# Seven products in the last dense chunk, and expert weight sums stored as plain blocks

## The chip, the cores and the metric

The kernel runs on one core of a Trainium2 chip. The metric is the device time of one execution in microseconds (us), as the median of several runs. The engines are TensorE (PE, matmuls), VectorE (DVE), ScalarE (ACT), GpSimd (POOL) and SyncE (SP, which here issues nearly all DMAs). Each engine works through its own list of instructions in order.

## The reference

Everything is fp32. An attention with packed keys is followed by a dense layer pair and a mixture of eight experts with a gating that is normalised in eight rounds. Sizes: 2304 tokens (4 batches of 576), model width 512, dense width 2048, 8 experts of width 1024.

```python
p_packed = sm_attn(p, k, v)                  # 4 x 8 heads, 32 packed keys
x = sm_attn(q, p_packed, p_packed)           # -> 2304 x 512
h = x @ w_in                                 # 512 -> 2048
x = (h * (1.0 / (1.0 + np.exp(-h)))) @ w_out # 2048 -> 512
logits = x @ w_gate
P = np.exp(logits - logits.max())
for _ in range(8):
    P /= P.sum(1, keepdims=True) + 1e-09
    P /= P.sum(0, keepdims=True) + 1e-09
    P *= N / E
for e in range(E):
    out += P[:, e:e + 1] * (np.maximum(x @ w1[e], 0.0) @ w2[e])
```

## The kernel before

**Precision.** PE multiplies numbers of a shortened fp32 format. Each operand is split into a high part (a cast on ACT) and a rest (a subtraction on DVE); that pair is the helper `split`, L145 and L146. A product of two operands is then three matmuls: high by high, high by rest, rest by high.

**Dense stage.** The dense width is cut into four chunks c of 512. Within a chunk the four batches b follow each other. For each batch `make_u` computes u (PE, L251) and splits it into Uh (ACT, L637) and Ul (DVE, L638). `gemm1` multiplies it with the attention's factors a2h and a2l: units g of 2 x 6 = 12 matmuls of 288 columns (L652), silu on ACT into `graw` (L683), and a split into the buffer `ring` (L684, L685). `gemm2_wide` multiplies ring by the split weights woh and wol: 24 tiles per chunk (2 batch pairs x 3 column ranges x 4 row blocks), each of 12 matmuls of 384 columns (L736). Half of the tiles are seeded with the running sum x2a or x2b by ACT (L721) and copied out by ACT (L741); the other half are added to x2 by DVE (L743). `convs` loads the next chunk's raw weights (win, rawin, ct, rawout; L519 on SP) and converts them on ACT and DVE (L528 to L546): the custom operation L539 ends the conversion of a w_out block. The work of this stage has the order of the code on PE, DVE and ACT (`tc.manual_schedule`).

**Expert weights.** The expert stage has 48 steps: 3 token groups by 16 weight blocks (8 experts x 2 halves). Group 0 (256 tokens) is computed plainly. Groups 1 and 2 (1024 tokens each) use Strassen and Winograd's scheme: seven products in place of eight, on quarter blocks of w1 and w2, of which four need sums of quarters. `pre_w1` computes the four sums S_1 to S_4 of each of the 16 weight blocks on DVE (L851) out of two raw blocks r of 512 KB, splits them into tiles po, and stores each with both parts (512 KB) to the DRAM tile w1d (L841, on SP). It is a generator: `pump_pre` takes `RATE[c]` pieces of it per unit of weight, where a g unit counts 0.8 and a wide tile 2 + 2/15. In the same way `pump_conv` takes pieces of the conversion. The generator runs through chunks 1, 2 and 3; `pre0` then splits the first step's tokens (xs) and weights (w1l, w2l). Behind chunk 3 comes lg, the gating product (L1235).

**Groups 1 and 2.** `moe_step` interleaves up products (12 matmuls of 512 columns, L1201, accumulators X, Z and Y) with down products d (12 matmuls, L1153) of the step before: 7 slots of 24 matmuls per step. `w1_get` fetches the weights of the product that comes `AHEAD` = 3 slots later: for the products 1, 2 and 4 the raw quarter `rb` (256 KB, loaded ahead by `w1_block`) is split, for 6, 7, 5 and 3 the stored pair is loaded from w1d as one DMA of 512 KB, tile w1l.

Of the kernel before, what the change touches and what calls it, by code (L numbers as in the profile page):

```python
# [28 lines left out]
RATE = {1: 36 / 64, 2: 36 / 64, 3: 41 / 53}  # L29
CONV = 0.6  # L30
TW = 384
LATE = 3
AHEAD = 3

# [71 lines left out]
def fused_kernel(  # L106
# [134 lines left out]
    win, wout = {}, {}  # L241
# [270 lines left out]
    def conv2(c, kind, j):  # L512
# [393 lines left out]
    def w1_block(s, p, name="rb"):  # L906
        _, e, fh = steps[s]
        t = st[name].tile([128, 2, 256], F32, tag=name, name=f"rb{s}_{p}")
        r, c = 256 * (p != 1), FH * fh + 256 * (p == 4)
        nc.sync.dma_start(t, w1[e, r:r + 256, c:c + 256].rearrange("(c p) f -> p c f", p=128))  # L910
        raw1[s, p] = t

    def w1_get(s, p):
        if p not in (1, 2, 4):
            wf[s, p] = get(w1d, s, p)
        else:
            t = unit([128, 2, 2, 256], F32R, f"w1f{s}_{p}")
            split(t[:, 0], t[:, 1], raw1.pop((s, p)))
            wf[s, p] = t
# [642 lines left out]
```

## Time and profile before

| what | value |
|---|---|
| time, median of 3 runs | 1785.59 us (1784.74 to 1787.44) |
| time of the profiled execution | 1784.47 us |
| its span, first to last instruction | 1782.7 us |
| chunks 1 to 3 of the dense stage end at | 369.96 us |
| last g unit and wide tiles of chunk 3 | 354.28 to 369.96 us |

The span is what the trace covers; 1.8 us of the execution's time lie around it. All starts in the rows below are counted from the start of the span. A group of rows in the trace joins instructions of one line, engine, operation and tile; its mean is the duration of one instruction, and since neighbours on an engine overlap a little, the distance between two starts can be shorter than the mean.

### The profile page before, as it was taken

The numbers are of one execution on the slowest core, as the hardware profiler recorded it, in microseconds if no ns is written. First come the engines' busy times: TensorE is split into PE (matmuls) and PEld (weight loads), VectorE is DVE, ScalarE is ACT, GpSimd is POOL, SyncE is SP. The second block draws the span as 40 slices with busy tenths as digits, with TensorE's granted clock in tenths as the row PEclk, the third lists the DMA queues.
The fourth block names the chain that finished last, engine by engine and source line by source line (L and its number), as shares of the span: only waits on it lengthen the run. The fifth ranks groups of instructions, "written<-read, shape, count | busy, mean of one in ns | idle before, by whom it ended". The sixth has DMA issues, their size and how long they took to land.

```text
span 1782.7 us, 25352 instructions
## 1 busy us (share of the span) xinstructions
PE 1764.3 (99%) x9564; PEld 1506.0 (84%) x9564; DVE 1438.8 (81%) x1918; ACT 1066.4 (60%) x1694; POOL 1.0 (0%) x8
## 2 busy tenths in 40 slices
PE   7999999999999999999999999999999999999998
PEld 4999999989998888888888888888888888888887
DVE  7868796759676988999889999887777777777778
ACT  6776675644454666665666666656555555555555
POOL 0000000000000000000000000000000000000000
PEclk9999999999999999999999999999999999999999
DMA  9326676875664655465544455964454444445432
GB/s 353 139 95 214 245 263 249 329 258 172 221 209 161 229 181 183 160 203 187 197 163 171 172 187 195 324 221 166 156 174 164 155 154 148 170 155 171 148 130 94
DMA packets 141498, 341.75 MB, mean 192 GB/s; under 512 B 11952, under 2 KB 49472, under 8 KB 140480
## 3 DMA queue, kind: packets, MB, share of 16 engines
q1 hardware_dynamic: 141376, 340.14, 54.7%
q8 instruction: 75, 1.23, 0.3%
q14 instruction: 47, 0.39, 0.1%
HBM read 256.66 MB, written 83.44 MB: 191 GB/s over the span
## 4 chain that ended last, share of the span: by engine, by line
PE 95%; DVE 2%; DMA 2%; ACT 1%; issue 0%; SPq 0%; DVEq 0%; ACTq 0%
PE d L1153 34%; PE X L1201 20%; PE Z L1201 10%; PE g2w L736 8%; PE g L652 5%; PE Y L1201 5%; PE u L1046 5%; PE d L1065 4%; PE g L704 3%; DMA v<-in_v_dram 1%; PE u L251 1%; DMA kq<-in_kT_dram 0%; PE pp L367 0%; PE s L251 0%; PE lg L1235 0%
## 5 line engine op out<-in xcount | busy, mean ns | idle before, releaser
L146 DVE TENSOR_TENSOR lo<-hb,hi 128x1024 fp32r<-128x1024 f32 x224 | 273.5, 1221 | 33.4 <-ACT hi L145 32.3
L1153 PE MATMUL d<-hi,w2f 128*128 128x512 f32 x896 | 294.2, 389 | 0.0
L1201 PE MATMUL X<-xf,w1l 128*128 128x512 f32 x1152 | 276.9, 389 | 0.0
L145 ACT CAST hi<-hb 128x1024 fp32r<-128x1024 f32 x224 | 235.4, 1052 | 64.9 <-PE d L1153 59.6
L1201 PEld LDWEIGHTS X<-xf,w1l 128*128 128x128 f32 x1152 | 216.2, 188 | 44.9
L1161 ACT COPY M<-d 128x512 f32<-128x512 f32 x234 | 137.4, 589 | 143.9 <-PE d L1153 140.7
L1165 DVE TENSOR_TENSOR M<-d,M 128x512 f32<-128x512 f32 x204 | 140.1, 687 | 100.8 <-PE d L1153 100.8
L1153 PEld LDWEIGHTS d<-hi,w2f 128*128 128x128 f32 x896 | 168.1, 188 | 34.9
L1153 PE MATMUL d<-lo,w2f 128*128 128x512 f32 x448 | 174.3, 389 | 0.0
L1153 PE MATMUL d<-hi,w2l 128*128 128x512 f32 x512 | 167.8, 389 | 0.0
L736 PE MATMUL g2w<-ring,woh 128*128 128x384 f32 x576 | 147.6, 337 | 0.0
L1149 ACT COPY d<-M 128x512 f32<-128x512 f32 x216 | 127.1, 589 | 21.1 <-DVE M L1165 19.7
L1153 PE MATMUL d<-hi,w2g 128*128 128x512 f32 x384 | 125.7, 389 | 0.0
L1153 PEld LDWEIGHTS d<-hi,w2l 128*128 128x128 f32 x512 | 96.1, 188 | 20.3 <-ACT d L1149 0.4
L736 PEld LDWEIGHTS g2w<-ring,woh 128*128 128x128 f32 x576 | 102.9, 188 | 8.6 <-issue 7.5
L1208 ACT COPY cp<-X 128x512 f32<-128x512 f32 x128 | 74.7, 583 | 47.2 <-PE X L1201 47.1
L1153 PE MATMUL d<-lo,w2l 128*128 128x512 f32 x256 | 99.6, 389 | 0.0
L1153 PEld LDWEIGHTS d<-lo,w2f 128*128 128x128 f32 x448 | 84.1, 188 | 17.5
L1201 PE MATMUL Y<-xf,w1f 128*128 128x512 f32 x384 | 97.3, 389 | 0.0
L736 PE MATMUL g2w<-ring,wol 128*128 128x384 f32 x288 | 96.3, 334 | 0.0
L1046 PE MATMUL u<-xs,w1h 128*128 128x256 f32 x512 | 94.4, 285 | 0.0
L145 ACT CAST w1f<-rb 128x512 fp32r<-128x512 f32 x96 | 59.8, 624 | 55.8 <-PE d L1153 41.0
(219 smaller groups left out, 3469.0 us busy)
## 6 DMA issues: line engine op xcount, KB each, us to landing
r<-in_moe_w_dram SPq DMA_DIRECT2D x128, 512.0 KB, 4.0
w1l<-w1d SPq DMA_DIRECT2D x128, 512.0 KB, 4.0
w1d<-po SPq DMA_DIRECT2D x64, 512.0 KB, 4.5
w2d<-w2f SPq DMA_DIRECT2D x64, 512.0 KB, 4.0
w2l<-w2d SPq DMA_DIRECT2D x64, 512.0 KB, 3.5
rb<-in_moe_w_dram SPq DMA_DIRECT2D x96, 256.0 KB, 2.6
sb<-in_moe_w_dram SPq DMA_DIRECT2D x48, 256.0 KB, 2.7
pb<-pd SPq DMA_DIRECT2D x16, 512.0 KB, 4.9
```

What stands on the lines that cost most here:

```text
L145: act.copy(out=hi, in_=raw)
L146: eng.tensor_tensor(out=lo, in0=raw, in1=hi.bitcast(F32), op=ALU.subtract)
L652: pe.matmul(ps, lhs[:, fs], rhs, start=(n == 0), stop=(n == 5))
L736: pe.matmul(ps[:, :TW], lhs[:, f % 2, ds], ring[f // 2][:, 2 * (f % 2) + rhs, q], start=(n == 0 and not on), stop=(n == 11), skip_group_ch ...
L1046: pe.matmul(ps[:, i], w[:, k % 2, f], x[:, k], start=(n == 0), stop=(n == 11))
L1065: pe.matmul(ps, h[:, l, f % 2, 128 * tt:128 * tt + 128], w[:, f % 2], start=(fh == 0 and n == 0), stop=(fh == 1 and n == 11))
L1149: act.copy(out=ps, in_=m)
L1153: pe.matmul(ps, w[:, l, c, 128 * d:128 * d + 128], r[:, c], start=(n == 0 and not seed), stop=(n == 5), skip_group_check=seed)
L1161: act.copy(out=m, in_=ps)
L1165: dve.tensor_tensor(m, ps, m, op=ALU.add)
L1201: pe.matmul(ps, w[:, l, c, 128 * i:128 * i + 128], x[:, r, c], start=(n == 0 and p in (1, 7)), stop=(n == 5), skip_group_check=p in (2, 6, ...
L1208: act.copy(out=t, in_=ps)
```

## The change

There are three parts.

1. The second GEMM of the last dense chunk (c = 3) is computed by seven products per batch in place of the wide tiles. `g_unit` leaves silu's result as raw blocks of 288 columns; `forms_a`, `forms_b`, `forms_c` and `h_form` make sums of them and split them into the buffer `ft`, `w_forms` does the same with the weights (tiles wS, from `wz`, the converted blocks that are no longer split). `product` multiplies one form pair with 2 x 6 matmuls of 288 columns, in the accumulators X, Z and Y; X and Z are added to x2 by DVE twice or more as the accumulation goes on, Y is seeded and copied out by ACT.
2. `pre_w1` holds the raw blocks of two steps (tags r1 and rx), and stores each sum S as it is (256 KB) for 13 of the 16 steps; for the steps 0, 1 and 15 (`WHOLE`) it splits and stores pairs as before. It runs in chunks 1 and 2 only.
3. In groups 1 and 2 the products 6, 7, 5 and 3 of those 13 weight blocks get their weights from the stored sum alone: it is loaded as an `rb` block (256 KB, SP), ACT casts it to the high part and writes that part's negative into the rest, then a DMA from GpSimd's queue adds the stored sum to the rest (256 KB, L937). Three `rb` buffers in place of two.

The rates and the raw block without a split:

```diff
-RATE = {1: 36 / 64, 2: 36 / 64, 3: 41 / 53}
-CONV = 0.6
+RATE = {1: 34 / 64, 2: 35 / 64}
+CONV = {1: 0.6, 2: 0.8}
 TW = 384
 LATE = 3
 AHEAD = 3
+WHOLE = (0, 1, 15)
...
+            if c == NC - 1:
+                wz[j] = z.rearrange("p (k f) -> p k f", k=2)
+                return
```

The sums and their use:

```diff
-    def w1_form(s, p, x):
-        if p in (6, 5):
-            t = st["po"].tile([128, 2, 2, 256], F32R, tag="po", name=f"po{s}_{p}")
-        else:
-            t = unit([128, 2, 2, 256], F32R, f"po{s}_{p}")
+    def keep_sum(s, p, x):
+        w1d[s, p] = tc.dram_tile([128, 2, 256], F32, name=f"w1d{s}_{p}")
+        nc.sync.dma_start(w1d[s, p], x)
+    def keep_form(s, p, x):
+        t = unit([128, 2, 2, 256], F32R, f"po{s}_{p}")
         split(t[:, 0], t[:, 1], x)
         put(w1d, s, p, t)
-    def pre_w1(todo, then):
-        load_w1(todo[0], 0)
-        load_w1(todo[0], 1)
-        yield
-        yield
-        for s, nxt in zip(todo, todo[1:] + [then]):
-            forms_ = yield from sums4(s)
-            load_w1(nxt, 0)
-            load_w1(nxt, 1)
-            yield
-            yield
-            for p, x in forms_:
-                w1_form(s, p, x)
+    def pre_w1(todo):
+        for i in range(2):
+            for j in range(2):
+                load_w1(todo[i], j, ("r1", "rx")[i])
+        yield
+        yield
+        for i, s in enumerate(todo):
+            a11, a12, a21, a22 = (x for x in (
+                raw1[s, 0][:, :, 0:256], raw1[s, 1][:, :, 0:256],
+                raw1[s, 0][:, :, 256:512], raw1[s, 1][:, :, 256:512]))
+            s1 = sums(s, 1, ALU.add, a21, a22)
+            s2 = sums(s, 2, ALU.subtract, s1, a11)
+            yield
+            s3 = sums(s, 3, ALU.subtract, a11, a21)
+            s4 = sums(s, 4, ALU.subtract, a12, s2)
+            if s not in WHOLE:
+                keep_sum(s, 5, s1)
+                keep_sum(s, 6, s2)
+            nxt = todo[i + 2] if i + 2 < len(todo) else 0 if i % 2 == 0 else None
+            if nxt is not None:
+                load_w1(nxt, 0, ("r1", "rx")[i % 2])
+                load_w1(nxt, 1, ("r1", "rx")[i % 2])
+            yield
+            if s in WHOLE:
+                for p, x in ((5, s1), (6, s2), (7, s3), (3, s4)):
+                    keep_form(s, p, x)
+                    yield
+            else:
+                keep_sum(s, 7, s3)
+                keep_sum(s, 3, s4)
...
     def w1_block(s, p, name="rb"):
         _, e, fh = steps[s]
+        if s % G0 in WHOLE and p not in (1, 2, 4):
+            return
         t = st[name].tile([128, 2, 256], F32, tag=name, name=f"rb{s}_{p}")
         r, c = 256 * (p != 1), FH * fh + 256 * (p == 4)
-        nc.sync.dma_start(t, w1[e, r:r + 256, c:c + 256].rearrange("(c p) f -> p c f", p=128))
+        nc.sync.dma_start(t, w1[e, r:r + 256, c:c + 256].rearrange("(c p) f -> p c f", p=128)
+                          if p in (1, 2, 4) else w1d[s % G0, p])
         raw1[s, p] = t
     def w1_get(s, p):
-        if p not in (1, 2, 4):
+        if s % G0 in WHOLE and p not in (1, 2, 4):
             wf[s, p] = get(w1d, s, p)
+            return
+        t = unit([128, 2, 2, 256], F32R, f"w1f{s}_{p}")
+        raw = raw1.pop((s, p))
+        if p in (1, 2, 4):
+            split(t[:, 0], t[:, 1], raw)
         else:
-            t = unit([128, 2, 2, 256], F32R, f"w1f{s}_{p}")
-            split(t[:, 0], t[:, 1], raw1.pop((s, p)))
-            wf[s, p] = t
+            act.copy(out=t[:, 0], in_=raw)
+            act.activation(t[:, 1], t[:, 0].bitcast(F32), AF.Copy, scale=-1.0)
+            nc.gpsimd.dma_start(t[:, 1], w1d[s % G0, p], accum_op=ALU.add)
+        wf[s, p] = t
```

The last chunk (`minus` is a DVE subtraction, `forms_b` and `forms_c` are made like `forms_a`, with a form and a sum more; `o` is the order of the batches):

```diff
+    def w_forms():
+        while len(wz) < 2:
+            yield
+        a11, a21 = wz[0][:, :, 0:256], wz[0][:, :, 256:512]
+        a12, a22 = wz[1][:, :, 0:256], wz[1][:, :, 256:512]
+        ta, tb = (st["S"].tile([128, 2, 256], F32, tag="S", name=f"ws{n}") for n in "ab")
+        def form(p, x):
+            wS[p] = unit([128, 2, 2, 256], F32R, f"wS{p}")
+            split(wS[p][:, 0], wS[p][:, 1], x)
+        form(1, a11)
+        yield
+        dve.tensor_tensor(tb, a11, a21, op=ALU.subtract)
+        form(7, tb)
...
+        def g_unit(k, j, half):
+            if k not in box["raw"]:
+                box["raw"][k] = dict(zip((11, 12, 21, 22, 5), raw_set(k)))
+            ps = box["pg"].tile([128, 2, 512], F32, tag="pg", name=f"g1_{k}{half}{j}")
+            for i in range(2):
+                gemm1_mm(ps[:, i, :HS], c, o[k], half, 2 * j + i)
+            act.activation(box["raw"][k][10 * (j + 1) + half + 1], ps[:, :, :HS], AF.Silu)
...
+        def h_form(k, p, x):
+            if "ft" not in box:
+                box["ft"] = hp.tile([128, 4, 2 * S], F32R, tag="h0", name="ft")
+            t = box["ft"][:, fn[0] % 4].rearrange("p (l c s) -> p l c s", l=2, c=2)
+            fn[0] += 1
+            split(t[:, 0], t[:, 1], x)
+            box["f"][k, p] = t
...
+        def forms_a(k):
+            r = box["raw"][k]
+            h_form(k, 1, r[11])
+            minus(r[11], r[12], r[11])
...
+        CH = {1: "X", 6: "X", 5: "X", 3: "X", 7: "Z", 4: "Z", 2: "Y"}
+        OUT = {1: (0, 0), 6: (1, 0), 5: (1, 1), 3: (0, 1), 7: (1, 1), 4: (1, 0), 2: (0, 0)}
+        def acc_of(k, p, d):
+            dh, half = OUT[p]
+            b = o[k]
+            off = (b % 2) * S + half * HS
+            return x2[b // 2][2 * dh + d][:, off:off + HS]
+        def seed2(k):
+            for d in range(2):
+                box["Y", d] = box["p3"].tile([128, 512], F32, tag="y", name=f"sY{k}{d}")
+                act.copy(out=box["Y", d][:, :HS], in_=acc_of(k, 2, d))
+        def product(k, p):
+            w, t, ch = wS[p], box["f"].pop((k, p)), CH[p]
+            for d in range(2):
+                if p in (1, 7):
+                    box[ch, d] = box["p3"].tile([128, 512], F32, tag="y", name=f"s{ch}{k}{d}")
+                ps = box[ch, d][:, :HS]
+                n = 0
+                for f in range(2):
+                    for l, r in ((0, 0), (0, 1), (1, 0)):
+                        pe.matmul(ps, w[:, l, f, 128 * d:128 * d + 128], t[:, r, f],
+                                  start=(n == 0 and p in (1, 7)), stop=(n == 5),
+                                  skip_group_check=p not in (1, 7))
+                        n += 1
+                dst = acc_of(k, p, d)
+                if p == 2:
+                    act.copy(out=dst, in_=ps)
+                else:
+                    dve.tensor_tensor(dst, ps, dst, op=ALU.add)
+            step()
...
+        need(4)
+        g_unit(0, 0, 0)
+        wide()
+        g_unit(0, 0, 1)
+        wide()
+        wide()
+        wide()
+        forms_a(0)
+        g_unit(0, 1, 1)
+        make_u(c, o[1])
+        forms_b(0)
+        g_unit(0, 1, 0)
+        for k in range(4):
+            r, more = box["raw"][k], k < 3
+            if k == 1:
+                hr_st.close()
+                closers["rx"].close()
+                a2b_st.close()
+                open_("gh", 6)
+                open_("r2", 2)
+                load_w2(0, 0)
+                load_w2(0, 1)
+            product(k, 1)
+            if k == 0:
+                forms_c(0)
+                need(5)
+                h_form(0, 4, r[5])
+            if more:
+                g_unit(k + 1, 0, 0)
+            h_form(k, 5, r[11])
+            product(k, 7)
+            h_form(k, 2, r[21])
+            need(6)
+            product(k, 6)
+            if more:
+                g_unit(k + 1, 0, 1)
+            h_form(k, 3, r[22])
+            need(7)
+            product(k, 4)
+            if more:
+                forms_a(k + 1)
+                g_unit(k + 1, 1, 1)
+            seed2(k)
+            product(k, 5)
+            if more:
+                forms_b(k + 1)
+                g_unit(k + 1, 1, 0)
+            product(k, 2)
+            if k == 2:
+                cvn = pre0()
+            if more:
+                forms_c(k + 1)
+            if k < 2:
+                make_u(c, o[k + 2])
+            product(k, 3)
+            if more:
+                h_form(k + 1, 4, box["raw"][k + 1][5])
```

The expert stage:

```diff
+                q += 2
+                if q < 7 * NS:
                     w1_block(q // 7, ORD[q % 7])
...
+        for name, n in (("hb", 6), ("hi", 3), ("lo", 3), ("rb", 3)):
```

What stands where, at three places. The first is DVE in chunk 2, up to the Ul of the chunk's third batch. S are the sums of expert weights, r and rx their raw blocks, po their splits, ct and win the weights in conversion, x2a the running sum; ISA is the custom operation. Before:

```order
L851 TENSOR_TENSOR S_3_2849<-r_60_2704 128x512
L851 TENSOR_TENSOR S_4_2851<-r_61_2706,S_2_2832 128x512
L743 TENSOR_TENSOR x2a_788<-g2w_2874,x2a_788 128x384
L146 TENSOR_TENSOR po_6_2891<-S_2_2832,po_6_2891 128x512
L685 TENSOR_TENSOR ring_103<-graw,ring_103 128x2x288
L531 TENSOR_SCALAR ct_2888<-ct_2888 128x1024
L532 TENSOR_SCALAR ct_2888<-ct_2888 128x1024
L146 TENSOR_TENSOR po_7_2915<-S_3_2849,po_7_2915 128x512
L685 TENSOR_TENSOR ring_1745<-graw,ring_1745 128x2x288
L534 SCALAR_TENSOR_TENSOR ct_2888<-rawout_2758,ct_2888 128x1024
L638 TENSOR_TENSOR Ul_2948<-u_2938,Uh_2947 128x1024
L539 ISA ct_2888<-rawout_2758,ct_2888 128x2048
```

After:

```order
L855 TENSOR_TENSOR S_1_2933<-rx_2801,rx_2803 128x512
L855 TENSOR_TENSOR S_2_2935<-S_1_2933,rx_2801 128x512
L747 TENSOR_TENSOR x2a_788<-g2w_2937,x2a_788 128x384
L532 TENSOR_SCALAR ct_2930<-ct_2930 128x1024
L533 TENSOR_SCALAR ct_2930<-ct_2930 128x1024
L855 TENSOR_TENSOR S_3_2953<-rx_2801 128x512
L855 TENSOR_TENSOR S_4_2955<-rx_2803,S_2_2935 128x512
L689 TENSOR_TENSOR ring_103<-graw,ring_103 128x2x288
L535 SCALAR_TENSOR_TENSOR ct_2930<-rawout_2787,ct_2930 128x1024
L689 TENSOR_TENSOR ring_1749<-graw,ring_1749 128x2x288
L540 ISA ct_2930<-rawout_2787,ct_2930 128x2048
L642 TENSOR_TENSOR Ul_3015<-u_3005,Uh_3014 128x1024
```

Before the change the row ahead of Ul is a SCALAR_TENSOR_TENSOR and the custom operation stands behind Ul; after it the custom operation stands ahead of Ul, and two splits po have given way to sums S.

At the same place SP's queue after the change, where w1d is a stored sum, numbered by its product (S_3 goes to product 7, S_4 to 3):

```order
L827 DMA r_110_2891<-in_moe_w_dram 128x2x512
L827 DMA r_111_2893<-in_moe_w_dram 128x2x512
L860 DMA w1d_7_2911<-S_3_2883 128x512
L860 DMA w1d_3_2913<-S_4_2885 128x512
L860 DMA w1d_5_2957<-S_1_2933 128x512
L860 DMA w1d_6_2959<-S_2_2935 128x512
L827 DMA rx_2961<-in_moe_w_dram 128x2x512
L827 DMA rx_2963<-in_moe_w_dram 128x2x512
L860 DMA w1d_7_2983<-S_3_2953 128x512
L860 DMA w1d_3_2985<-S_4_2955 128x512
```

The two raw blocks of a step stand between the stores of its sums S_1, S_2 and those of S_3, S_4; there are four S buffers, so a step's sums take the buffers of the sums of the step before.

The second place is DVE in chunk 3, first batch, after the change. ft are the split forms of h, L1488 the sums of raw blocks, L1537 the additions of an accumulator to x2b, Ul the second batch's:

```order
L147 TENSOR_TENSOR ft<-raw_3487,ft 128x576
L1488 TENSOR_TENSOR raw_3487<-raw_3488,raw_3487 128x576
L642 TENSOR_TENSOR Ul_3604<-u_3594,Uh_3603 128x1024
L1488 TENSOR_TENSOR raw_3488<-raw_3490,raw_3488 128x576
L147 TENSOR_TENSOR ft<-raw_3488,ft 128x576
L1488 TENSOR_TENSOR raw_3491<-raw_3490,raw_3487 128x576
L1537 TENSOR_TENSOR x2b_1373<-sX_3625,x2b_1373 128x288
L1537 TENSOR_TENSOR x2b_1374<-sX_3633,x2b_1374 128x288
L147 TENSOR_TENSOR ft<-raw_3491,ft 128x576
L1488 TENSOR_TENSOR raw_3491<-raw_3489,raw_3491 128x576
L147 TENSOR_TENSOR wS_3644<-ct_3051,wS_3644 128x512
L147 TENSOR_TENSOR ft<-raw_3491,ft 128x576
```

Ahead of the change ring splits of L685, po splits and the wide tiles' additions of 384 columns stood here. The Ul of the third batch stands 22 rows below the last row shown.

The third place is ACT in a step of group 1 after the change. rb is the loaded sum, w1f the pair of parts, d and M belong to the down product, w2f to w2:

```order
L935 CAST w1f_6_11032<-rb_6_10936 128x512
L936 ACTIVATE w1f_6_11032<-w1f_6_11032 128x512
L146 CAST w2f_7_11059<-S_3_11055 128x512
L1168 COPY d_11038<-M_6809 128x512
L1180 COPY M_6758<-d_10987 128x512
L935 CAST w1f_7_11086<-rb_7_10980 128x512
L146 CAST hi_3_11092<-hb_10921 128x1024
L936 ACTIVATE w1f_7_11086<-w1f_7_11086 128x512
```

The rows L935 and L936 are new; each pair is followed on GpSimd's queue by a DMA from w1d into w1f (L937), where before SP had a load of w1l from w1d (L845).

## Rows read from the trace of the kernel before

**Rows 1.** The page: busy time of each engine, and the chain that ended last.

```profile
PE 1764.3 (99%) x9564; PEld 1506.0 (84%) x9564; DVE 1438.8 (81%) x1918; ACT 1066.4 (60%) x1694; POOL 1.0 (0%) x8
...
PE 95%; DVE 2%; DMA 2%; ACT 1%; issue 0%; SPq 0%; DVEq 0%; ACTq 0%
```

**Rows 2.** Waits of TensorE: engine, line, releaser; us in total, times, longest.

```profile
PE s L251 <- DMA kq<-in_kT_dram: 10.7, 2, 10.5
PE pp L367 <- DMA v<-in_v_dram: 0.7, 1, 0.7
...
PE g L652 <- DVE Ul L638: 0.5, 2, 0.4
```

**Rows 3.** Chain of work, 280 to 400 us: start, us, what, matmuls.

```profile
292.99 1.02 PE u L251 x16
...
354.28 3.19 PE g L652 x24
357.47 12.49 PE g2w L736 x72
369.96 4.44 PE lg L1235 x56
```

**Rows 4.** Stretches: us, busy time (instructions) by engine, granted clock, DMA share, GB/s.

```profile
205.00:282.45 77.45, 77.07 (x519) 72.59 (x518) 61.56 (x87) 53.78 (x89) 0.00 (x0) 1.00 0.62 230
285.63:370.00 84.37, 84.37 (x556) 81.11 (x557) 57.94 (x93) 52.91 (x98) 0.00 (x0) 1.00 0.80 295
683.00:721.00 38.00, 38.00 (x170) 31.45 (x169) 34.43 (x47) 24.06 (x38) 0.00 (x0) 1.00 0.53 187
1254.00:1292.00 38.00, 38.00 (x170) 31.45 (x169) 28.93 (x37) 21.38 (x34) 0.00 (x0) 1.00 0.44 151
```

**Rows 5.** Timeline of DVE, 226 to 243 us: start, us, instruction.

```profile
229.01 0.69 DVE L532 TENSOR_SCALAR win<-win 128x1024 uint32<-128x1024 uint32 x1
229.62 0.68 DVE L146 TENSOR_TENSOR po<-S,po 128x512 fp32r<-128x512 f32 x1
230.22 1.22 DVE L534 SCALAR_TENSOR_TENSOR win<-rawin,win 128x1024 uint32<-128x1024 uint32 x1
...
240.96 1.22 DVE L638 TENSOR_TENSOR Ul<-u,Uh 128x1024 fp32r<-128x1024 f32 x1
242.09 1.21 DVE L539 CUSTOM_DVE_ANT_0 ct<-rawout,ct 128x2048 uint16<-128x2048 uint16 x1
```

**Rows 6.** Groups of DVE by shape, 270 to 375 us: busy us, mean ns, idle before.

```profile
L146 DVE TENSOR_TENSOR po<-S,po 128x512 fp32r<-128x512 f32 x30 | 19.7, 685 | 6.7 <-ACT po L145 6.7
L685 DVE TENSOR_TENSOR ring<-graw,ring 128x576 fp32r<-128x576 f32 x18 | 13.6, 758 | 15.6 <-ACT ring L684 15.6
L743 DVE TENSOR_TENSOR x2b<-g2w,x2b 128x384 f32<-128x384 f32 x11 | 6.1, 554 | 4.0 <-PE g2w L736 4.0
L638 DVE TENSOR_TENSOR Ul<-u,Uh 128x1024 fp32r<-128x1024 f32 x4 | 4.9, 1222 | 0.5 <-ACT Uh L637 0.5
...
L146 DVE TENSOR_TENSOR xs<-x2b,xs 128x128 fp32r<-128x128 f32 x4 | 1.1, 285 | 0.6 <-ACT xs L145 0.6
```

**Rows 7.** DMA issues, 285 to 370 us: count, KB each, median us to landing.

```profile
w1d<-po SPq DMA_DIRECT2D x26, 512.0 KB, 4.9
```

**Rows 8.** Timeline of TensorE at the g matmul that waited, 236 to 243.5 us.

```profile
242.23 0.40 PE L652 MATMUL g<-a2h,Ul 128*128 128x288 f32 x1 [0.38 <-DVE Ul L638]
```

**Rows 9.** DMA issues of the page: count, KB each, us to landing.

```profile
rb<-in_moe_w_dram SPq DMA_DIRECT2D x96, 256.0 KB, 2.6
```

**Rows 10.** The tile w1d, 130 to 370 us: landing of its 64 stores.

```profile
DMA to landing us min/median/max: 2.6/4.5/8.1
```

**Rows 11.** Groups of ScalarE by shape, one step of group 1 (683 to 721 us).

```profile
L145 ACT CAST w1f<-rb 128x512 fp32r<-128x512 f32 x3 | 1.9, 624 | 2.1 <-PE Z L1201 1.1 <-PE d L1153 1.0
```

**Rows 12.** Chain of work in the same step.

```profile
686.86 2.72 PE Z L1201 x12
```

**Rows 13.** Groups of DVE by shape in the same step.

```profile
L146 DVE TENSOR_TENSOR lo<-hb,hi 128x1024 fp32r<-128x1024 f32 x7 | 8.5, 1218 | 0.3 <-ACT hi L145 0.3
```

More of the change, by code (lines that the diff above doesn't have):

```diff
@@ L1348, in pump_pre @@
             due[0] -= 1
-            next(pre, None)
+            next(todo, None)
     def pump_conv(w):
-        due[1] += w * CONV
+        due[1] += w * CONV[c]
         if due[1] >= 1:
@@ L1355, in pump_conv, with pieces @@
             cvn.step()
+    wS = {}
+    def w_forms():
[12 more added lines that the diff above has]
+        yield
+        dve.tensor_tensor(ta, a21, a22, op=ALU.add)
+        form(5, ta)
+        yield
+        dve.tensor_tensor(ta, ta, a11, op=ALU.subtract)
+        form(6, ta)
+        yield
+        form(4, a22)
+        yield
+        dve.tensor_tensor(ta, a12, ta, op=ALU.subtract)
+        form(3, ta)
+        yield
+        form(2, a12)
+        yield
+    wf_ = w_forms()
+    def pieces():
+        yield from pre
+        while len(wS) < 4:
+            next(wf_)
+            yield
+    todo = pieces()
     tiles = []
@@ L1389, in fused_kernel @@
                 gemm1(c, b, half, pump)
-                if half == 1 and nxt is not None and not first:
+                if half == 1 and not first:
                     if nxt[0] != c:
@@ L1396, in fused_kernel @@
                 keep = {0: 2, 1: 2, 2: 2, 3: 4}[unit_]
-                if (c, b) == seq[NC][:2]:
+                if first:
                     keep = len(tiles)
-                if nxt is None and half == 1:
-                    keep = 0
                 while len(tiles) > keep:
@@ L1403, in fused_kernel, with step @@
                     gemm2_wide(*n, tiles[1] if len(tiles) > 1 else None, pump)
-                    if n == (NC - 1, order[c][2] // 2, 0, 3):
-                        for _ in pre:
-                            pass
-                        cvn = Rot([pre0()], 1)
-        cvn.drain()
+        cv_st.close()
+        c, o = NC - 1, order[NC - 1]
+        cvn = iter(())
+        hr, hr_st = pool("hr", 1, side="right", reuse_waits="tile")
+        box["raw"], box["f"] = {}, {}
+        fn = [0]
+        def step():
+            next(cvn, None)
@@ new lines, in raw_set @@
+        def raw_set(k):
+            if k == 0:
+                return [hr.tile([128, 2, HS], F32, tag=f"r{n}", name=f"raw{n}") for n in range(5)]
+            if k == 1:
+                box["rt"] = hp.tile([128, 8, 2, HS], F32, tag="h1", name="rawt")
+            if k == 2:
+                return [box["rt"][:, n] for n in (5, 6, 7)] + \
+                    [gt.tile([128, 2, HS], F32, tag="graw", name=f"raw2{n}") for n in range(2)]
+            return [box["rt"][:, n] for n in range(5)]
+        def g_unit(k, j, half):
[5 more added lines that the diff above has]
+            act.activation(box["raw"][k][10 * (j + 1) + half + 1], ps[:, :, :HS], AF.Silu)
@@ new lines, in forms_b, with forms_c @@
+        def forms_b(k):
+            r = box["raw"][k]
+            minus(r[12], r[22], r[12])
+            h_form(k, 7, r[12])
+            minus(r[5], r[22], r[11])
+        def forms_c(k):
+            r = box["raw"][k]
+            h_form(k, 6, r[5])
+            minus(r[5], r[21], r[5])
+        CH = {1: "X", 6: "X", 5: "X", 3: "X", 7: "Z", 4: "Z", 2: "Y"}
[5 more added lines that the diff above has]
+            return x2[b // 2][2 * dh + d][:, off:off + HS]
@@ L1411, in moe_step @@
+        for _ in cvn:
+            pass
     def moe_step(s):
```

59 lines of the change are left out of this document (24 added, 35 removed).

## The prediction

> **What bounds the kernel now.** I first read the page's busy shares and its chain of work that ended last: TensorE is busy for 99% of the span and holds 95% of the chain [rows 1]. Since a busy share is an average, the waits of PE came next: 10.7 us at the start, where the keys are awaited, and after them no line with more than 0.7; 0.5 of it at g matmuls that wait for Ul, a result of VectorE [rows 2]. So only two things can move the time: less work on PE, or new waits of PE. For the first, the chain between 280 and 400 us gives a price per matmul [rows 3]. For the second, the table of stretches says how much room VectorE (DVE) and ScalarE (ACT) have [rows 4]: in chunk 2 (205 to 282 us) DVE works 61.56 of 77.45 us, in chunk 3 57.94 of 84.37, in a 38 us step of group 1 34.43. DVE is the engine to watch everywhere. The granted clock is 1.00 in every stretch, so it cancels out.
>
> **PE's own work.** In chunk 3 the 24 wide tiles go: 24 x 12 = 288 matmuls of 384 columns. In their place come 4 batches x 7 products x 12 = 336 matmuls of 288 columns. The row of 72 wide matmuls gives 12.49/72 = 173.5 ns each, that of 24 g matmuls of 288 columns 3.19/24 = 132.9 ns [rows 3]. 288 x 173.5 = 49.96 us go, 336 x 132.9 = 44.66 us come: **-5.3 us**. The first GEMM of the chunk and PE's rows in the expert stage stay as they are, so this is all that can be gained. It is gained only if PE waits no more than before.
>
> **Chunk 3, first batch.** The forms of h and the additions into x2 fall to DVE, and PE's third-batch unit g_200 needs an Ul behind them. The order puts 34 DVE rows from the last wide tile to that Ul: 18 of 576 elements, 10 additions of 288 columns, 4 of 512, 2 of 1024. Rows of DVE that stand back to back start 0.08 us sooner than the mean duration says (the 512 row at 229.62 is followed 0.60 us later [rows 5]), so from [rows 6] I take 0.675 for 576, 0.60 for 512, 1.14 for 1024. No row has an addition of 288 columns from PSUM; it lies between the 128 and the 384 columns' rows (0.285 and 0.554 [rows 6]), nearer the latter, and I take 0.46, less 0.08 = 0.37. Sum: 12.15 + 3.7 + 2.4 + 2.28 = 20.5 us, with the wide tile's own addition 21.0. Thirteen of the rows are splits of forms, which wait for a cast on ACT; ring's 18 splits stood idle 15.6 us in all, 0.87 each [rows 6]. About seven come right behind the subtraction that makes their input, so 6.1 us more: 27.1 us. PE's work over the same rows is six g units and eight products of 12 matmuls (14 x 1.595 = 22.3) and two u of 1.02 [rows 3]: 24.4 us. **+2.7**, with a split or two more or less 2 to 4; I take 3.0. If all casts were hidden behind the additions it would be nothing (21.0 < 24.4).
>
> **Second and third batch: 0.** A batch costs DVE about the same 20 us, but the forms are made a batch ahead and PE has seven products and four g units between; X, Z and Y take PSUM tiles that have been free for a product. Before, chunk 3 hid 26 stores, their splits and their sums under the same PE time [rows 4, 7]; those are gone from here, which is the cover.
>
> **Last batch.** No g unit is left to lie between its products: 7 x 1.595 = 11.2 us of PE against 12 additions (4.4), four form splits (2.7), eight xs splits (1.6), four splits of 1024 for the experts (4.6) and two late additions (0.7), 14.0 us of DVE. The splits of w1 and w2 are wanted only after lg, whose 4.44 us [rows 3] cover the better part. **+1.5** (0 to 2.8).
>
> **Chunks 1 and 2.** All expert sums now run here, where before they went on through chunk 3: 26 of the 64 stores were issued there [rows 7]. As 13 steps lose their splits (four casts on ACT and four 0.6 us subtractions on DVE each), the load per chunk is about even; what changes is its shape. Take the Ul of chunk 2's third batch, the one that PE waited for [rows 8]; DVE ran without a pause up to it [rows 5]. From the Ul before to this one the old order has 31 rows: 12 of 512 elements, 6 TENSOR_SCALAR of 1024, 5 long operations (SCALAR_TENSOR_TENSOR or the custom one), 4 of 384 and 4 ring splits. The new one has 14, 4, 6, 4 and 4: ct's custom operation now stands ahead of Ul, not behind it. At starts 0.60, 0.62, 1.14, 0.47 and 0.675 apart [rows 5, 6] that is 21.2 us before and 22.3 after, and as PE waited already, the 1.1 us more is stall. Then there is a new wait. The four S buffers are now the source of the stores: S_3 of a step cannot be written before the store of the last step's S_3 has landed. That store is issued a piece after its sum, behind two raw blocks of 512 KB on SP's queue. At 34/64 and 35/64 of a piece per unit, a wide tile (2.13 units, 2.08 us) brings 1.15 pieces, a piece every 1.8 us, so two pieces (3.6 us) are left between store and next use. A transfer of 256 KB lands in 2.6 us as a median [rows 9]; a megabyte of raw blocks ahead of it takes 3 to 4 us at the 230 to 295 GB/s of these stretches [rows 4], and stores of 512 KB have landed in 2.6 to 8.1 us here, 4.5 in the middle [rows 10]. So the wait is 0 to 2.5 us, thirteen times, and everything behind it on DVE waits too: ring, x2 and Ul. Most falls into DVE's 16 us of room in such a chunk [rows 4]; what PE sees is what is late when an Ul is due, once a batch. At the Ul above I take 1.1 + 2 for one such wait, and at one other, the first of chunk 2, the 2 us of such a wait alone: **+5** (0 if stores land in time and the 1.1 is made up, 9 with two waits more).
>
> **Groups 1 and 2.** 26 of 32 steps get four weights each by a load of the stored sum (256 KB), two ACT operations and an accumulating DMA of the same size that GpSimd issues, instead of one load of 512 KB. ACT pays 8 x 0.624 = 5.0 us per step (its w1f cast [rows 11]; the second one is of the same 128x512), so 29.1 of 38 us in group 1 and 26.4 in group 2 [rows 4]. That leaves room; if it did not, ACT's copies of d would be late, and the down products with them. The accumulating DMA has no row before. From w1_get to use there are three slots of 24 matmuls, 3 x (2.72 + 2.72) = 16.3 us [rows 12], less about 2 for the two ACT operations ahead of it. The nearest rows are 256 KB loads, 2.6 us [rows 9], and from above the slowest 512 KB store, 8.1 [rows 10], as an accumulation reads two sides and writes one. Both are well under 14, so **0**; a landing over 14 us would stall PE 104 times.
>
> A rule speaks against this part. While DVE runs an operation in a two-port mode, says the Trainium skill ("SBUF — State Buffer", section "Who interferes with whom"), GpSimd cannot write descriptors, and a DMA issued from there starves; it exempts tensor_tensor. By the first half 34 us of DVE in a step would leave such DMAs almost no time; by the second nearly none of it counts, as the step's larger DVE rows are tensor_tensor, the longest group 8.5 us of them [rows 13]. No run here shows either yet. From the same skill's fit for GpSimd's DMAs ("DMA: Bandwidth & Descriptors", section "Anatomy of one DMA") I estimate 2.6 us for 256 KB, which would also make this term 0.
>
> **Sum.** -5.3 + 3.0 + 1.5 + 5 + 0 = +4.2. Against the profiled execution (span 1782.7, 1784.47 in all) that is 1788.7; the median of the runs, 1785.59, lies 1.1 above that execution, by which the median would be 1789.8. Since part of that distance is scatter, I put it at **1789.5**. Some 0.2% (3.6 us) is what a measurement of this kernel can tell from no change, so this lies at the edge of slower.
>
> **Rivals.**
> (a) *The stalls stay hidden.* ACT casts run ahead of DVE, stores land in under 3.6 us. For it: PE waited only 0.5 us at an 80% loaded DVE, and the splits that go were DVE and ACT work. Against it: four sums in a row are lumps that the old order did not have. 1785.6 - 5.3 = 1780.3, faster.
> (b) *Only chunk 3's waits are real.* If stores land in time, chunks 1 and 2 add a microsecond or two: -5.3 + 4.5 + 1.5 = +0.7, about 1786, the same.
> (c) *Forecast*: stores and lumps in chunks 1 and 2 as well, 1789.5. It turns into (b) where a store of 256 KB takes less than 3.6 us with its queue ahead of it.
> (d) *The accumulating DMAs are late*, starved or slow. If one holds their queue for more than 38/4 = 9.5 us they fall behind without end: at 11 us, 4 x 11 - 38 = 6 us in each of 26 steps, 156 us slower. Below 9.5 us and 14 us to landing it costs nothing. No row speaks for such a size.
>
> **How the numbers follow.** (a) 0.26, (b) 0.28, (c) 0.40, (d) 0.06. So faster 0.26, same 0.28, slower 0.46. The range goes from just under (a) to (c) with the upper ends of its terms, chunks 1 and 2 at 9 and chunk 3 at 6.8 (-5.3 + 15.8 = +10.5, 1796): 1779.5 to 1796, which leaves out (d) and the outskirts of (a).
>
> **What would show it.** The product rows at 133 ns and 336 of them (the 5.3 us). PE's waits: g on Ul at two or three batches in chunks 1 and 2, 1 to 3 us each; a wait of 1 to 2 us on Ul in chunk 3's third batch; product matmuls on ft of 0.2 to 0.7. DVE's waits: S sums released by stores. POOL: DMA landings well under 14 us, and no PE wait at L1220. I am wrong if PE's waits in chunks 1 to 3 together stay under 3 us, or if matmuls in the expert stage wait for w1f.

## The result and the profile after

The changed kernel takes 1806.24 us (median of 4 runs, 1805.81 to 1807.03) against 1785.57 before: ratio 1.0115, 95% interval [1.0097, 1.0132]. It is slower, as forecast, but by 20.7 us and not by 4, and outside the range.

The page's busy times and its chain, after (as [rows 1]):

```profile
PE 1766.5 (98%) x9612; PEld 1505.7 (83%) x9612; DVE 1445.8 (80%) x1939; ACT 1150.4 (64%) x1859; POOL 91.6 (5%) x112
...
PE 86%; DMA 6%; DVE 5%; ACT 1%; issue 1%; SPq 0%; DVEq 0%; ACTq 0%
```

The chain has moved off PE: 6% DMA and 5% DVE where there were 2% and 2%, although the shares of busy time are nearly those of before. The waits of PE in the dense stage (120 to 400 us), in the columns of [rows 2]:

```profile
PE g L656 <- DVE Ul L642: 17.7, 4, 8.8
PE g2w L740 <- DVE ring L689: 2.0, 3, 1.0
PE sZ L1529 <- DVE x2b L1537: 0.5, 1, 0.5
```

Before, Ul cost 0.5 us. The waits of DVE in the same stretch have a new head, the landing of the plain sums' stores:

```profile
DVE S L855 <- DMA w1d<-S: 30.0, 11, 6.0
DVE x2b L747 <- PE g2w L740: 12.2, 4, 6.8
DVE ft L147 <- ACT ft L146: 11.1, 11, 1.9
```

Where the time went is read from two starts on PE in the chain of work: u of the first batch of chunk 3, and lg behind that chunk. Before:

```profile
277.04 1.02 PE u L251 x16
```

(lg at 369.96, [rows 3]), and after:

```profile
300.38 1.09 PE u L252 x16
...
392.14 4.44 PE lg L1254 x56
```

So chunks 1 and 2 end 23.34 us later; chunk 3 takes 91.76 us in place of 92.92, 1.16 less; from lg to the end of the span it is 1413.2 us in place of 1412.7, 0.4 more. The loss lies in chunks 1 and 2 alone.

DVE's timeline there, up to the first Ul of chunk 2 that PE waits for (start, us, instruction, idle before and its releaser):

```profile
197.49 1.22 DVE L550 TENSOR_TENSOR wol<-ct,woh 128x1024 fp32r<-128x1024 f32 x1
204.74 0.69 DVE L855 TENSOR_TENSOR S<-rx 128x512 f32<-128x512 f32 x1 [6.03 <-DMA w1d<-S]
...
207.85 0.68 DVE L855 TENSOR_TENSOR S<-r,r 128x512 f32<-128x512 f32 x1
208.56 0.69 DVE L855 TENSOR_TENSOR S<-S,r 128x512 f32<-128x512 f32 x1
209.17 1.22 DVE L642 TENSOR_TENSOR Ul<-u,Uh 128x1024 fp32r<-128x1024 f32 x1
```

and PE at the same place:

```profile
202.85 0.29 PE L656 MATMUL g<-a2l,Uh 128*128 128x288 f32 x1
210.45 0.61 PE L656 MATMUL g<-a2h,Ul 128*128 128x288 f32 x1 [7.31 <-DVE Ul L642]
210.85 0.44 PE L656 MATMUL g<-a2h,Uh 128*128 128x288 f32 x1
211.09 0.44 PE L656 MATMUL g<-a2l,Uh 128*128 128x288 f32 x1
```

DVE stands 6.03 us before the sum S_3 until the last step's S_3 has landed in DRAM, and Ul, a few rows further on in its list, is late with it. The chain has that store, issued at 196.71; the buffer was wanted 2.0 us later, at 198.71:

```profile
196.71 8.01 DMA w1d<-S
```

The landing of all 52 stores:

```profile
DMA to landing us min/median/max: 2.0/6.1/8.8
```

PE stops for 7.3 us, and its matmuls then follow each other at 0.24 us, not 0.13. The table of stretches says why (columns of [rows 4]):

```profile
206.00:208.00 2.00, 0.00 (x0) 0.00 (x0) 2.00 (x5) 0.00 (x0) 0.00 (x0) 0.65 0.64 218
208.00:210.40 2.40, 0.00 (x0) 0.00 (x0) 2.36 (x3) 0.00 (x0) 0.00 (x0) 0.50 0.83 201
210.40:214.00 3.60, 3.55 (x17) 3.56 (x17) 1.02 (x2) 0.72 (x2) 0.00 (x0) 0.58 0.84 323
214.00:216.00 2.00, 2.00 (x15) 2.00 (x14) 1.48 (x3) 1.59 (x3) 0.00 (x0) 1.00 0.57 172
...
264.00:268.00 4.00, 4.00 (x19) 4.00 (x18) 2.74 (x5) 1.32 (x2) 0.00 (x0) 0.50 0.60 200
```

While PE stood idle the granted clock fell to half (1.2 GHz), and PE worked on at half speed until about 213.5. The second long wait, 8.8 us at the Ul of the third batch, has the same tail from 263 to 268. Three of DVE's waits stand ahead of that Ul:

```profile
237.81 0.69 DVE L855 TENSOR_TENSOR S<-rx 128x512 f32<-128x512 f32 x1 [3.60 <-DMA w1d<-S]
...
248.09 0.69 DVE L855 TENSOR_TENSOR S<-r 128x512 f32<-128x512 f32 x1 [2.15 <-DMA w1d<-S]
...
257.14 0.69 DVE L855 TENSOR_TENSOR S<-rx 128x512 f32<-128x512 f32 x1 [4.11 <-DMA w1d<-S]
...
261.98 1.22 DVE L642 TENSOR_TENSOR Ul<-u,Uh 128x1024 fp32r<-128x1024 f32 x1
```

Some 8 us at half speed are 4 us lost; with the two waits (16.1), the wide tiles' waits for ring in chunks 1 and 2 (1.9) and 0.5 at an Ul of chunk 1, less the 0.5 of before, that makes 22 of the 23.3 us.

### The profile page after: what moved, and what is told of

Same layout as the page of the kernel before. It is cut to its first block, busy times and chain, and to the rows that moved or that the text cites. A ratio compares the mean times of both kernels' runs of the same rounds, so it can differ in the third digit from the quotient of the medians.

```text
span 1805.3 us, 25881 instructions
## 1 busy us (share of the span) xinstructions
PE 1766.5 (98%) x9612; PEld 1505.7 (83%) x9612; DVE 1445.8 (80%) x1939; ACT 1150.4 (64%) x1859; POOL 91.6 (5%) x112
## 4 chain that ended last, share of the span: by engine, by line
PE 86%; DMA 6%; DVE 5%; ACT 1%; issue 1%; SPq 0%; DVEq 0%; ACTq 0%
PE d L1172 33%; PE X L1220 19%; PE Z L1220 10%; PE Y L1220 5%; PE u L1065 5%; PE d L1084 4%; DMA w1d<-S 4%; PE g L656 3%; PE g L708 3%; DVE S L855 1%; PE g2w L740 1%; DMA v<-in_v_dram 1%; PE sX L1529 1%; DMA vt<-in_v_dram 1%; PE u L252 0%
## 5 line engine op out<-in xcount | busy, mean ns | idle before, releaser
L1220 PE MATMUL X<-xf,w1f 128*128 128x512 f32 x1320 | 317.0, 389 | 0.0
L1220 PEld LDWEIGHTS X<-xf,w1f 128*128 128x128 f32 x1320 | 247.7, 188 | 51.5
L937 POOL DMA_DIRECT2D w1f<-w1d x104 | 90.7, 872 | 1622.2 <-DVE cp L1243 634.7
L1220 PE MATMUL Z<-xf,w1f 128*128 128x512 f32 x696 | 167.3, 389 | 0.0
L1220 PEld LDWEIGHTS Z<-xf,w1f 128*128 128x128 f32 x696 | 130.6, 188 | 27.1
L740 PE MATMUL g2w<-ring,woh 128*128 128x384 f32 x384 | 99.2, 338 | 2.0 <-DVE ring L689 2.0
```

Of the source, the lines that this page charges most:

```text
L740: pe.matmul(ps[:, :TW], lhs[:, f % 2, ds], ring[f // 2][:, 2 * (f % 2) + rhs, q], start=(n == 0 and not on), stop=(n == 11), skip_group_ch ...
L937: nc.gpsimd.dma_start(t[:, 1], w1d[s % G0, p], accum_op=ALU.add)
L1220: pe.matmul(ps, w[:, l, c, 128 * i:128 * i + 128], x[:, r, c], start=(n == 0 and p in (1, 7)), stop=(n == 5), skip_group_check=p in (2, 6, ...
```

## The experiments

**Are the waits for stores the cause?** Theory W: DVE's waits for the landing of stores reach PE at the two Ul. Rival L: the new order of rows on DVE and late transfers are enough. The first run takes the waits away by another source, a tile of zeros (the stored sums are then zeros, so this run does not compute the result):

```diff
+        box["sc"] = st["sc"].tile([128, 2, 256], F32, tag="sc", name="sc")
+        nc.gpsimd.memset(box["sc"], 0.0)
...
-        nc.sync.dma_start(w1d[s, p], x)
+        nc.sync.dma_start(w1d[s, p], box["sc"])
```

> The stores of plain sums read a tile that is written once, so no sum waits for a store's landing; the number and size of DMAs and DVE's rows are those of the changed kernel (the stored sums are zeros, so four of the seven products of the expert groups work on zeros). Theory W (DVE waits for the landing of stores, 30.0 us in 11 waits, and its lateness reaches PE at two Ul): the waits go, PE's waits of 7.3 and 8.8 us at Ul fall under 2 us each, the granted clock stays 1.00, and the time is 1783 to 1787 us. Rival L (the order of sums and conversions on DVE, and transfers that are late for any reader, are enough): PE still waits more than 10 us and the time stays above 1798 us.

1785.33 us, ratio 1.0007 [0.9998, 1.0017]; all of the loss is gone, and the clock is 1.00 in every stretch of chunks 1 to 3. PE's waits for Ul:

```profile
PE g L656 <- DVE Ul L642: 4.0, 4, 1.9
```

But this run does more than was meant: as a constant can be stored at once, SP issued all these stores before 200 us, so that chunk 2 had less traffic too. It does not tell the waits from the traffic. Two runs change the order and the number of buffers, and one does both:

```diff
             if s not in WHOLE:
-                keep_sum(s, 5, s1)
-                keep_sum(s, 6, s2)
+                for p, x in ((5, s1), (6, s2), (7, s3), (3, s4)):
+                    keep_sum(s, p, x)
...
-        for name, n in (("S", 4), ("r1", 2), ("rx", 2)):
+        for name, n in (("S", 5), ("r1", 2), ("rx", 2)):
```

> All four stores of a step are issued right behind its sums, ahead of the raw blocks; four S buffers as in the changed kernel. Theory W: the stores of S_3 and S_4 come a piece earlier and not behind a megabyte, they land in about 4 us after issue, DVE's waits fall from 30 us to under 12 and the time to 1786 to 1795 us. Rival Q (the transfers themselves are near their limit, so what the stores gain the raw blocks lose): DVE waits for raw blocks instead, the time stays within 4 us of 1806.

> One S buffer more (five), the order of stores unchanged. Each sum now takes the buffer of the sum before it in the last step, S_3 that of S_2, whose store goes out a piece earlier and ahead of the raw blocks; S_4 that of S_3. Theory W: waits fall by half, to 10 to 18 us, and the time to 1790 to 1799 us. Rival L: no change, 1804 to 1808 us.

> Both: the stores ahead of the raw blocks and five S buffers. Theory W: DVE waits under 5 us, the time 1783 to 1788 us, at or a little above the kernel without waits for stores. Rival Q: above 1798 us, with waits for raw blocks.

Stores ahead: 1798.01 us [1.006, 1.009]. Five buffers: 1804.94 [1.0098, 1.0128]. Both: 1797.57 [1.0055, 1.0088]. DVE's waits for stores, in this order:

```profile
DVE S L855 <- DMA w1d<-S: 11.2, 8, 3.7
```

```profile
DVE S L855 <- DMA w1d<-S: 22.2, 9, 6.5
```

```profile
DVE S L855 <- DMA w1d<-S: 7.7, 4, 5.0
```

The waits fell as expected of the first (under 12 us), and PE's at Ul with them, from 17.7 to 10.8; the time came out 3 us above the expectation. The other two missed. With five buffers DVE's waits fell by a quarter, but PE's waits for Ul stayed (18.2 us): the waits between the second batch's Ul and the third's came to 10.4 us (2.8, 1.2 and 6.5) where they had been 9.9. With both edits DVE still waits 7.7 us for stores, and 5.0 of them fall ahead of the first Ul of chunk 2, 2.2 (with 0.9 for a raw block) ahead of the third. PE waits 5.5 and 3.6 us there, the granted clock is 0.50 behind both, and the time is 10 us above the expectation. DVE's waits for raw blocks, which rival Q looks for, are there but small (1.7 us). What counts is not the sum of DVE's waits but those ahead of an Ul.

**The stores at their place, without a wait.** The four sums are written into the quarters that they are made of; three raw blocks take turns, and the next load waits on SP:

```diff
-            s1 = sums(s, 1, ALU.add, a21, a22)
-            s2 = sums(s, 2, ALU.subtract, s1, a11)
+            dve.tensor_tensor(a22, a21, a22, op=ALU.add)
+            dve.tensor_tensor(a21, a11, a21, op=ALU.subtract)
             yield
-            s3 = sums(s, 3, ALU.subtract, a11, a21)
-            s4 = sums(s, 4, ALU.subtract, a12, s2)
+            dve.tensor_tensor(a11, a22, a11, op=ALU.subtract)
+            dve.tensor_tensor(a12, a12, a11, op=ALU.subtract)
...
+                load_q(todo[i + 2], sets[(i + 2) % 3])
```

> The whole change, but the four sums are written into the raw block that they are made of, and three raw blocks take turns (r1, rx and the four S buffers), so DVE never waits for a store; a raw block's load waits for the stores on SP's queue instead. Theory W (the landing of stores was what cost 21 us): no DVE wait for a store, granted clock 1.00 throughout chunks 1 to 3, PE's waits at Ul together under 5 us, 1783 to 1787 us, as where the stores read a constant tile (1785.33). Rival Q (the queue is too full, the wait only moves from the stores to the raw blocks): DVE waits for raw blocks by 10 us and more, time above 1792 us.

1789.93 us, ratio 1.0028 [1.0017, 1.0039]: 16 of the 21 us are back with the same bytes to store, but 3 us more than expected are left. DVE has one long wait in the stretch, for a raw block, and PE waits for it and 1.2 us more, with half speed behind (the profile is of the longest of the seven executions, 1791.69 us):

```profile
238.31 0.69 DVE L894 TENSOR_TENSOR q<-q,q 128x512 f32<-128x512 f32 x1 [3.48 <-DMA q<-in_moe_w_dram]
...
246.38 1.22 DVE L642 TENSOR_TENSOR Ul<-u,Uh 128x1024 fp32r<-128x1024 f32 x1
```

```profile
247.65 0.61 PE L656 MATMUL g<-a2h,Ul 128*128 128x288 f32 x1 [4.69 <-DVE Ul L642]
```

So rival Q holds to a part: the queue is full enough for a raw block to come late. Its transfers are also in smaller packets here (59% of them under 2 KB from 130 to 290 us, against 8% in the changed kernel), which this design brings with it.

**Is there room on DVE ahead of that Ul?** The 25 us up to it, in the kernel before and then in the run with the constant source:

```profile
218.00:243.00 25.00, 24.62 (x163) 23.16 (x163) 23.66 (x34) 16.79 (x27) 0.00 (x0) 1.00 0.76 262
```

```profile
218.00:243.00 25.00, 25.00 (x166) 24.00 (x166) 24.79 (x36) 15.66 (x24) 0.00 (x0) 1.00 0.68 249
```

DVE worked 23.66 of 25 us before and 24.79 without waits for stores: 1.3 and 0.2 us of room. Batch by batch, from the end of one Ul of chunk 2 to the start of the next, the kernel before has these stretches ahead of the first, second and third Ul (columns of [rows 4]; the first starts at the last Ul of chunk 1):

```profile
178.70:198.26 19.56, 19.56 (x135) 18.55 (x134) 18.55 (x28) 14.99 (x25) 0.00 (x0) 1.00 0.92 320
199.50:216.90 17.40, 17.40 (x122) 16.40 (x121) 9.02 (x14) 12.33 (x21) 0.00 (x0) 1.00 0.57 210
218.10:240.96 22.86, 22.86 (x153) 21.62 (x152) 21.52 (x33) 16.79 (x27) 0.00 (x0) 1.00 0.75 255
```

DVE's room there is 1.0, 8.4 and 1.3 us. In the changed kernel its waits for stores in the same stretches are 8.4 us (1.3, 1.1 and 6.0), 5.7 (2.6 and 3.2) and 9.9 (3.6, 2.2 and 4.1). Waits less room give 7.4, nothing and 8.5 us; PE waited 7.3, nothing and 8.8. This is an estimate and no full account, since the new order also has 1.7 and 1.5 us more of DVE's work ahead of the first and third Ul. The waits ahead of the second Ul cost PE nothing; of those ahead of the first and third nearly all but the room reaches PE.

Two runs move work in this stretch. One takes the changed kernel and issues the pieces that fall due in a batch's second g units behind the next Ul, which puts 2.3 us of conversion (L535 and the custom L540) behind the third batch's:

```diff
-                gemm1(c, b, half, pump)
+                held = []
+                gemm1(c, b, half, held.append if half == 1 and not first else pump)
...
                     make_u(*nxt)
+                for w in held:
+                    pump(w)
```

> The changed kernel with the same edit alone: the stores and their waits stay. If the waits for stores make most of the loss and the order ahead of Ul only the 1.1 to 2.3 us that its rows take, the time falls by 1 to 5 us (two Ul, 2.3 us each at most) to 1801 to 1805 us. If the order of the rows ahead of Ul were the main cause, it would fall below 1795 us.

1802.94 us [1.0089, 1.0116], as expected: 3.3 less than the changed kernel by the medians, 2.3 by the ratios to the kernel before, whose intervals overlap. DVE still waits 29.0 us for stores. The order of the rows is worth a few microseconds at most, the waits the rest.

**Chunk 3: the products and their stalls.** The same sums in place, with the wide tiles of before:

> The same sums in place and the new path of expert weights, but chunk 3 with the wide tiles of before (no seven products). By the sum of the prediction the products bring -5.3 + 4.5 = -0.8 us, so this is 0.8 us above the kernel with products: 1784 to 1788 us, and the stretch from chunk 3's first g unit to lg is 87.5 us. Rival P (the products keep their whole gain): 4 to 5.5 us above. Rival N (the products are a loss by their forms): more than 1 us below.

1792.06 us [1.0027, 1.0052], 2.1 above the one with products, between the forecast 0.8 and rival P; the range of 1784 to 1788 was missed, since the sums in place themselves cost more than expected. By the chain of work u stands here at 284.39 and lg at 377.31:

```profile
284.39 1.02 PE u L252 x16
...
377.31 4.44 PE lg L1267 x56
```

That is 92.92 us, to the hundredth the 92.92 of before; with the products it is 91.69 in place (285.25 to 376.94). So the products as they stand bring 1.2 us of their 5.3; the last batch's chain in the changed kernel shows how they lose there:

```profile
381.34 0.40 DVE xs L147 x2
381.74 0.67 DVE ft L147
382.41 0.73 DVE x2a L1537 x2
383.14 0.40 DVE xs L147 x2
383.54 0.67 DVE ft L147
```

Each product costs DVE 0.73 (two additions) + 0.40 (two xs splits) + 0.67 (a form) = 1.80 us, where PE needs 1.60. Three runs try the terms, from the kernel with sums in place. First w1's splits go to the batch before, then the third batch's Ul earlier as well:

```diff
-        yield from w1_split(0)
...
+            if k == 2:
+                cvn = w1_split(0)
...
             product(k, 5)
+            if k == 0:
+                make_u(c, o[2])
...
-            if k < 2:
+            if k == 1:
                 make_u(c, o[k + 2])
```

> The sums in place, and the two splits of the first expert step's w1 go from the last batch of chunk 3 to the batch before (2.3 us of DVE and 2.0 of ACT). By the term of the last batch (14.0 us of DVE against 11.2 of PE, 1.5 us lost) DVE then has 11.7 us there, and 0.5 to 1.5 us come back: 0.5 to 1.5 below the kernel with the sums in place alone. Rival: the last batch waits for the accumulators' additions one by one, not for DVE's sum of work: no change (under 0.3).

> As the one before, and the third batch's u and Ul are made one g unit and one product earlier in the first batch of chunk 3. By the term of the first batch (3.0 us, of which 1.1 showed at that Ul) another 0.5 to 1.5 us come back. Rival: DVE is behind with all of the first batch's work, so that the forms of the second batch are late instead: no change.

By their medians both are within the scatter of chunk 2's waits (1790.71 and 1790.02 us, [1.0019, 1.0042] and [1.0018, 1.0042]), so chunk 3 is read from the chain: u to lg 91.68 us (284.19 to 375.87) and 90.73 (282.03 to 372.76). The splits of w1 brought nothing, the rival; the earlier Ul 0.95 us. Then xs behind the last product, and with it the raw blocks' loads a piece earlier:

```diff
             a11, a12, a21, a22 = quart[s]
+            if i + 2 < len(todo):
+                load_q(todo[i + 2], sets[(i + 2) % 3])
...
-        for _ in cvn:
+        for _ in pre0():
             pass
```

> Sums in place with the raw block of two steps later loaded a piece earlier (ahead of the step's own stores), w1's splits and the third batch's Ul early as in the runs before, and the eight xs splits behind the last product. Theory (one wait of DVE in the full stretch of chunk 2 passes on to PE whole, and in the last batch DVE's 1.8 us per product bind): DVE's wait of 2.5 to 3.5 us for a raw block goes and with it 4 to 6 us; the last batch's products run at 1.6 us each, 0.8 to 1.5 us less: 1783 to 1786 us. Rival: the raw blocks are late wherever they are issued, since the queue is full: DVE waits for them by 3 us or more and the time stays above 1788 us.

1785.66 us, ratio 1.0005 [0.9996, 1.0014]. In the profiled execution DVE has no wait of over 1 us for a store or a block ahead of chunk 2's Ul (one of 3.5 us comes behind the last of them), and PE waits 2.6 us for Ul in all, 2.1 of it at the third, ahead of which DVE's own wait is 0.8. That execution took 1783.49 us, one of the two shortest of eleven; what the median one does with 2.2 us more no profile shows. The last batch's products:

```profile
360.73 1.61 PE sX L1544 x12
362.34 1.60 PE sZ L1544 x12
363.94 1.60 PE sX L1544 x12
```

They run at PE's own pace, and u to lg takes 89.49 us (279.25 to 368.74): 1.24 us less, as expected.

**Versions.** With the sums' pieces shifted to chunk 1, and with the held pieces on top of the last version:

```diff
-RATE = {1: 34 / 64, 2: 35 / 64}
+RATE = {1: 39 / 64, 2: 30 / 64}
```

> As the one before, with the pieces of the sums at 39/64 per unit in chunk 1 and 30/64 in chunk 2. If it is the lack of room on DVE ahead of chunk 2's third Ul that costs, fewer sums there take away its last wait (0.5 to 4 us of PE) and nothing is lost in chunk 1: 1782 to 1785 us. If the faster pieces make chunk 1's blocks late, DVE waits for raw blocks or stores there and the time is above 1787 us.

> As the kernel with blocks loaded early and xs late, and the pieces of sums and conversion that fall due in a batch's second g units are issued behind the next batch's Ul, so that 2.3 us of conversion (a SCALAR_TENSOR_TENSOR and the custom operation) no longer stand ahead of chunk 2's third Ul. If DVE has no room ahead of that Ul, PE's waits of 2.1 and 0.5 us there go to nearly nothing and the time is 1781.5 to 1784.5 us, below the kernel before. Rival: lateness of raw blocks moves the wait to another place and the time stays at 1785 to 1788 us.

1789.48 us [1.0015, 1.0033] and 1786.30 [0.9999, 1.0017]. Both missed, and the other branch of each expectation came. In the first, DVE waits at the end of chunk 1 for a store (1.9 us at 201.76) and in chunk 2 for another (1.4), and PE for 6.1 us at Ul in all; this profile is of the longest of eleven executions (1792.07 us). In the second a raw block is 3.4 us late at 237.16, and PE waits 5.1 us from 160 to 290 us, at ring and graw (3.9) and at Ul (1.2). That the edit moved the wait there, as its rival said, is likely but not shown, since the profile of the version without it is of one of its shortest executions. None of the versions beats the kernel before.

## Why the prediction was wrong

- **PE's own work, -5.3 us: right.** The 336 matmuls of the products run at 1.60 us per 12, 133 ns each.
- **Chunk 3, +4.5 us: right in size, partly wrong in make.** Forecast -0.8 net, measured -1.16. The third batch's Ul, made in the first, was late as said (PE waited 1.1 us). The last batch lost 1.4 us (its chain from 376.36 to lg is 15.8 us for nine products of 1.60), not by the sum of DVE's work with w1's splits but by 1.80 us of DVE per product against 1.60 of PE; moving the splits of w1 did nothing, moving xs gave 1.24 us. In the best version 1.9 us of the chunk's stalls are left (89.49 against 92.92 - 5.3), which no run takes apart.
- **Groups 1 and 2, 0: right.** The accumulating DMAs land like this:

```profile
DMA to landing us min/median/max: 3.9/5.4/8.4
```

The bounds were 2.6 and 8.1, the upper one just passed, the deadline 14; no matmul waits for w1f. A step of group 1 has ACT at 28.68 of 38 us (29.1 forecast), DVE at 34.99, and PE at 38.00. GpSimd spends 0.87 us on the issue of each. By the Trainium skill ("SBUF — State Buffer", section "Who interferes with whom") GpSimd's descriptors can starve beside two-port operations of DVE, and did not beside tensor_tensor. The trace agrees with the second half, with landings of 5.4 us in the middle and 8.4 at most beside a DVE that is busy for 92% of the step, most of it with tensor_tensor; no run here tests the first half. The estimate of 2.6 us from the Trainium skill's fit ("DMA: Bandwidth & Descriptors", section "Anatomy of one DMA") is half of what an accumulation took here; the measurement decides.
- **Chunks 1 and 2, +5 us: this step failed.** It cost 23.3 us. The place (the third Ul of chunk 2, and the first, which was named without a reason) and the mechanism (a sum waits for the store of the last step's sum, and Ul behind it) were right. Three terms were not.
  - *The size of a wait.* It was put at 0 to 2.5 us, thirteen times; there are eleven, 2.7 us on average, six of them over 2.5 and one 6.0. Part of this is a slip in the sum: a megabyte at 230 to 295 GB/s takes 3.6 to 4.6 us and not 3 to 4, so that by the prediction's own rows a store lands after 6.2 to 7.2 us and the wait is 2.6 to 3.6. The stores on the chain took 5.8 to 8.8 us, 6.8 in the middle. The other part is the time between store and next use, 3.6 us by the mean pace of pieces, but 2.0 at the wait of 6.0.
  - *What of the waits reaches PE.* "Most falls into DVE's 16 us of room in such a chunk", with one wait of 2 us left at each of two Ul. That room is a sum over 77 us, and most of it lies ahead of the second Ul, where PE waits for nothing, and behind the fourth. Ahead of the first and third it was 1.0 and 1.3 us, against waits of 8.4 and 9.9, and PE got 7.3 and 8.8.
  - *The clock.* It was taken to cancel out, being 1.00 in every stretch of the kernel before. Behind the two waits PE ran at 1.2 GHz for some 8 us, 4 us more.
- The 1.1 us for the order of rows ahead of Ul is borne out in kind: 2 to 3 us for two Ul with 2.3 us moved at the third. Rivals (a) and (b), in which the stores land in time, are out: DVE waits 30.0 us for them. Rival (d) did not happen.

What stays open: how low chunks 1 and 2 can get with the stores spread out differently. The best version that computes everything ends 2.2 us later there than before and gains 3.4 us in chunk 3, in one of its shortest executions; by all its runs it is the same as the kernel before.

## What to carry to other kernels

When an engine that works in order gets a wait, look for room in the rows just ahead of the instruction that another engine waits for, not in the mean of the stage: a stage in which DVE was idle for 20% of the time had 5% there. A buffer that a DMA store reads is free when the store has landed, so count landing with the queue ahead of it against the time to the buffer's next use, and compute into memory that is wanted again late, or let the queue's issuer wait in place of the compute engine. Work per item on the second engine (1.80 us) against the first (1.60) tells more than sums over a batch.

## What was not expected of the hardware

The granted clock fell from 1.00 to 0.50 within PE's idle times of 7.3 and 8.8 us and stayed there for 3 to 5 us of work behind them (and some 6 us behind the idle time of 4.7 us with the sums in place); it stayed at 1.00 through an idle time of 1.9 us in the run with a constant source. An accumulating DMA of 256 KB issued by GpSimd took 5.4 us to land, where plain loads of that size in the same stage took 2.6 (rb from w1d).
